# A retention kernel with a bilinear feed-forward: the first load of q and of k as two DMAs each

## The chip, the cores and the metric

The kernel runs on 1 core of one Trainium2 chip. The metric is the device time of one execution in microseconds. Before the change it is 325.2 us, the median of 3 runs (325.12 to 325.22).

## The reference

```
q, k, v: [8 batches, 8 heads, 576 positions, 64]
scores = (1 / 8) * q @ k.T                             # per batch and head
gamma[h] = 1 - 2 ** (-5 - h)
D[h, i, j] = gamma[h] ** (i - j) where i >= j, else 0
attn = (scores * D[h]) @ v
x = attn with the heads side by side                   # [4608 tokens, 512]
out = ((x @ w_a) * (x @ w_b)) @ w_out                  # w_a, w_b: 512 x 1536, w_out: 1536 x 512
```

There is no softmax, so the decay factors can be pulled apart into one factor per query and one per key, and the keys of earlier positions can be folded into a state (k.T @ v).

## The kernel before

The whole of the work runs on one core in an order that is written out by hand. The feed-forward part goes over the tokens in blocks (512, 256, 256, then 512 each). For a block it makes `pa = x @ w_a` (line 794), which ACT copies to `ha` (line 802), and `pb = x @ w_b` (line 809), which DVE multiplies with `ha` to `hT` (line 814), and then `po = hT @ w_out` (line 828). Retention work for later tokens is put between the matmuls of these blocks through a list of due times.

Before the first block there is an opening. It handles the first 256 positions of batches 0 and 1 in four steps, each of one batch and four heads: `STEPS` (line 165) makes step 0 the heads 0 to 3 of batch 0, step 1 the heads 0 to 3 of batch 1, step 2 the heads 4 to 7 of batch 0, and step 3 the heads 4 to 7 of batch 1. For a step, `load_step` (line 154) brings q, k and v in float32 into `qf`, `kf` and `vf`: 128 partitions, two neighbouring positions and four heads in each, 256 KB. `cast_step` (line 311) makes them bfloat16 (`qkb`) on the engine named in the call, one instruction over all four heads; `values_step` (lines 319 and 321) multiplies v by a factor per key; `transpose_step` (line 329, copies in line 333) turns q and k; `score_step` (line 347, masked in line 355) makes the scores; `state_step` (line 374, copies in lines 386 to 391) makes the states; the output steps (lines 421, 437, 448) make `xT`, the input of the feed-forward part. `make_qs` (line 223) makes tables of factors on ACT. `warm` (line 855) issues matmuls on a tile of ones whose result nobody reads. POOL issues the weight loads (lines 264, 266, 269) between its casts. The first feed-forward matmuls on half a block are in `ffn_begin` and `begin_with` (line 771).

The loads of the four steps are the first instructions of the program. They are issued in this order, all from SP except the first k, which ACT issues:

```python
    for i, which in ((0, Q), (0, K), (0, V), (2, Q), (2, K), (1, K),
                     (1, Q), (2, V), (3, K), (3, Q), (1, V), (3, V)):
        load_step(*STEPS[i], which,
                  nc.scalar if (i, which) == (0, K) else nc.sync)
```

Behind its load of k, ACT makes the factors of the keys (line 213) and two of the tables; the four steps then run as lines 860 to 920 list them, in the order 0, 2, 1, 3. DVE casts q and k of step 0, POOL casts those of step 2 and the k of steps 1 and 3, ACT casts the q of steps 1 and 3. Every DMA has a completion semaphore; the program uses eight for the DMAs of SP and ACT, in turn, and a DMA that takes one for the second time waits for the one that had it before.

Of the kernel before, what the change touches and what calls it, by code (L numbers as in the profile page):

```python
# [18 lines left out]
def kernel(  # L19
# [10 lines left out]
    nc = tc.nc  # L30

    B, H, S, D = q.shape
    DM = H * D
# [104 lines left out]
    paired = {}  # L138
# [12 lines left out]
                    src[b, :, s0:s0 + m, :].rearrange("h s d -> s h d"))  # L151
            paired[n][i] = t

    def load_step(n, hh, which, on=nc.sync):

        if n not in paired:
            paired[n] = [stage.tile([128, 2 * DM], FP32, tag=name, name=name)
                         for name in ("qf", "kf", "vf")]
        on.dma_start(  # L159
            paired[n][which][:, hh * DM:(hh + 1) * DM]  # L160
            .rearrange("p (h e) -> p h e", h=4),
            (q, k, v)[which][n, 4 * hh:4 * hh + 4, 0:256, :]
            .rearrange("h (p two) d -> p h (two d)", two=2))

    STEPS = [(0, 0), (1, 0), (0, 1), (1, 1), (2, 0), (2, 1)]
    Q, K, V = 0, 1, 2
    for i, which in ((0, Q), (0, K), (0, V), (2, Q), (2, K), (1, K),
                     (1, Q), (2, V), (3, K), (3, Q), (1, V), (3, V)):
        load_step(*STEPS[i], which,
                  nc.scalar if (i, which) == (0, K) else nc.sync)  # L170

# [757 lines left out]
    for i, which in ((4, Q), (4, K), (4, V), (5, Q), (5, K), (5, V)):  # L931
        load_step(*STEPS[i], which)
# [135 lines left out]
```

## Time and profile before

| | |
|---|---|
| time, median of 3 runs | 325.2 us |
| the profiled execution: its own time | 325.43 us |
| its span | 323.7 us |
| PE busy | 314.0 us (97%) |
| DVE, ACT, POOL busy | 165.4, 131.5, 118.8 us |
| moved by DMA | 50.90 MB, mean 157 GB/s |
| DMAs of `qf` from SP, 256 KB each | 32, median 4.7 us from issue to landing |
| granted TensorE clock | 1.00 |

The span is counted from the first to the last instruction of the core; 1.73 us of the profiled execution's own time lie around it. PE, DVE, ACT and POOL are the tensor, vector, scalar and GpSimd engines, PEld the weight loads of PE, SP the engine that only issues and waits. SPq and ACTq are the issuing of DMAs on SP and ACT, which is not counted as busy time. L12 is line 12 of the kernel before. In a timeline a row gives the start in us, the duration, the engine, the line, what is written and read, the shapes, and in brackets how long the engine was idle just before and what ended that. In a table of stretches each row has the stretch, its length, the busy time of PE, PEld, DVE, ACT and POOL (with the number of instructions), the granted clock, the mean busy share of the 16 DMA engines (it can pass 1 where packets overlap) and GB/s. A busy PE is not a PE at its peak.

### The profile page before, as it was taken

The page shows a single profiled execution, that of the slowest core. Times are in us where ns is not written, and L with a number is a line of the kernel's source. Part 1 is how long each engine was busy: PE and PEld are TensorE (multiplying, and loading weights), DVE is VectorE, ACT ScalarE, POOL GpSimd, SP SyncE. Part 2 cuts the span into 40 slices and gives each one's busy share as a digit, 9 for nine tenths or more (in the row PEclk, how much of TensorE's full clock was granted, in tenths as well). Part 3 has the DMA queues.
Part 4 walks back from the last instruction along what each step waited for, and adds up shares of the span by engine and source line. Part 5 has one row for each costly group of instructions (what it writes and reads, how often), then busy time and mean ns, then how long its engine had stood idle before and what let it go on. Part 6 is the DMA issues. An engine that isn't in the chain of part 4 may idle for free.

```text
span 323.7 us, 8631 instructions
## 1 busy us (share of the span) xinstructions
PE 314.0 (97%) x3573; PEld 164.4 (51%) x3611; DVE 165.4 (51%) x294; ACT 131.5 (41%) x293; POOL 118.8 (37%) x158
## 2 busy tenths in 40 slices
PE   7899999999999999999999999999999999999996
PEld 3564457778444554444454545454445444444444
DVE  5744445665546754835374626562566256514321
ACT  7735753463435523533253324442433343313321
POOL 4990077574755274447165305450530000000000
PEclk9999999999999999999999999999999999999999
DMA  8999999999999999999999169935840520031013
GB/s 216 255 196 207 259 231 189 200 176 206 174 221 223 195 208 206 269 222 263 175 197 216 52 163 198 207 74 144 194 86 19 104 76 2 2 97 32 1 23 108
DMA packets 145431, 50.90 MB, mean 157 GB/s; under 512 B 126704, under 2 KB 140912, under 8 KB 145392
## 3 DMA queue, kind: packets, MB, share of 16 engines
q1 hardware_dynamic: 140112, 45.37, 68.4%
q0 software_dynamic: 4752, 4.72, 8.8%
q8 instruction: 28, 0.46, 0.6%
q10 hardware_dynamic: 528, 0.26, 0.3%
q14 instruction: 11, 0.09, 0.1%
HBM read 37.75 MB, written 9.44 MB: 146 GB/s over the span
## 4 chain that ended last, share of the span: by engine, by line
PE 92%; DMA 2%; SPq 2%; ACT 1%; issue 1%; DVE 1%; DVEq 0%
PE pb L809 29%; PE po L828 29%; PE pa L794 28%; DMA qf<-in_q_dram 2%; SPq L159 2%; PE sc L600 1%; PE o L628 1%; PE o L641 1%; PE kv L538 1%; PE pa L771 1%; ACT state_after L386 0%; ACT vb L319 0%; PE tp L329 0%; DVE hT L814 0%; ACT own L390 0%
## 5 line engine op out<-in xcount | busy, mean ns | idle before, releaser
L814 DVE TENSOR_TENSOR hT<-ha,pb 128x512 bf16<-128x512 bf16 (+1 forms) x120 | 75.9, 633 | 94.8 <-PE pb L809 86.6
L802 ACT CAST ha<-pa 128x512 bf16<-128x512 f32 (+1 forms) x120 | 64.8, 543 | 115.9 <-PE pa L794 109.9
L809 PE MATMUL pb<-xT,wb_sb 128*128 128x512 bf16 (+1 forms) x474 | 111.2, 357 | 0.5
L794 PE MATMUL pa<-xT,wa_sb 128*128 128x512 bf16 (+1 forms) x452 | 106.9, 356 | 1.2 <-issue 0.6
L828 PE MATMUL po<-wo_sb,hT 128*128 128x512 bf16 (+2 forms) x442 | 94.7, 367 | 1.7 <-issue 1.4
L809 PEld LDWEIGHTS <-wb_sb 128*128 128x128 bf16 x480 | 47.0, 98 | 46.6 <-issue 0.3
L794 PEld LDWEIGHTS <-wa_sb 128*128 128x128 bf16 x468 | 45.0, 98 | 44.4 <-issue 0.2
L828 PEld LDWEIGHTS <-hT 128*128 128x128 bf16 x456 | 42.7, 98 | 47.2
L484 POOL CAST qkb<-qf 64x1024 bf16<-64x1024 f32 x15 | 15.5, 1031 | 64.4 <-DMA qf<-in_q_dram 55.1
L495 POOL TENSOR_TENSOR vb<-vf,vs 128x1024 bf16<-128x1024 f32 (+1 forms) x17 | 28.9, 1700 | 13.3 <-DMA vf<-in_v_dram 6.1
L839 DVE COPY osb<-po 128x512 f32<-128x512 f32 (+2 forms) x17 | 11.1, 653 | 43.0 <-PE po L828 43.0
L837 ACT COPY osb<-po 128x512 f32<-128x512 f32 (+1 forms) x21 | 12.0, 573 | 43.4 <-PE po L828 40.5
L484 POOL CAST qkb<-kf 64x1024 bf16<-64x1024 f32 (+1 forms) x17 | 16.4, 966 | 16.7 <-DMA kf<-in_k_dram 16.5
L563 DVE TENSOR_TENSOR sums<-kv,sums 128x256 f32<-128x256 f32 x44 | 18.7, 424 | 2.8 <-PE kv L538 0.8
L609 DVE TENSOR_TENSOR sT<-sc,mask 128x512 bf16<-128x512 f32 x30 | 19.4, 681 | 0.0
L488 POOL CAST qkb<-kf 64x512 bf16<-64x512 f32 (+1 forms) x34 | 18.7, 579 | 1.0
L488 POOL CAST qkb<-qf 64x512 bf16<-64x512 f32 x30 | 17.6, 615 | 0.6
L567 ACT CAST states<-sums 64x512 bf16<-64x512 f32 x26 | 16.0, 617 | 0.3
L654 DVE TENSOR_TENSOR xT<-o,qs 128x512 bf16<-128x512 f32 x24 | 15.4, 682 | 1.5 <-PE o L641 1.5
L311 POOL CAST qkb<-kf 128x512 bf16<-128x512 f32 x5 | 3.1, 617 | 16.9 <-DMA kf<-in_k_dram 16.9
L355 DVE TENSOR_TENSOR sT<-sc,mask_s 128x1024 bf16<-128x1024 f32 x6 | 7.2, 1222 | 1.3 <-PE sc L347 1.2
L855 PE MATMUL w<-ones 128*128 128x512 bf16 x17 | 6.3, 482 | 1.5 <-DVE idxp_f L204 1.5
(88 smaller groups left out, 163.5 us busy)
## 6 DMA issues: line engine op xcount, KB each, us to landing
qf<-in_q_dram SPq DMA_DIRECT2D x32, 256.0 KB, 4.7
vf<-in_v_dram SPq DMA_DIRECT2D x32, 256.0 KB, 5.2
kf<-in_k_dram SPq DMA_DIRECT2D x31, 256.0 KB, 4.8
out_dram<-osb SPq DMA_DIRECT2D x25, 256.0 KB, 3.2
out_dram<-osb SPq DMA_DIRECT2D x21, 128.0 KB, 2.6
wo_sb<-in_moe_w_out_dram POOLq DMA_DIRECT2D x3, 512.0 KB, 16.7
qf<-in_q_dram SPq DMA_DIRECT2D x8, 128.0 KB, 3.2
kf<-in_k_dram SPq DMA_DIRECT2D x8, 128.0 KB, 3.5
```

The lines of the kernel that those rows point to most:

```text
L484: nc.gpsimd.tensor_copy(qkb[0:64, w, e], t[0:64, e])
L488: nc.gpsimd.tensor_copy(to[:, :, 1 - r], fro[:, :, r])
L495: nc.gpsimd.tensor_tensor(vb[:, e].rearrange("p (h d) -> p h d", d=D), t[:, e].rearrange("p (h d) -> p h d", d=D), decay[:, at], op=ALU.mult)
L563: nc.vector.tensor_tensor(sums[:, i], own, prev, op=ALU.add)
L567: nc.scalar.copy(to(half(1 - r)), fro(half(r)))
L609: nc.vector.tensor_tensor(sT[:, on].rearrange("p c k s -> p (c k) s"), sc[:, on].rearrange("p c k s -> p (c k) s"), mask3.unsqueeze(1).to_ ...
L654: nc.vector.tensor_tensor(x_of(t0, 128).rearrange("p c (a s) -> p c a s", a=2), o[:, :, :, kp].rearrange("p a c s -> p c a s"), qs[:, :, s ...
L794: nc.tensor.matmul(pa[:, 0:n], wa_sb[:, c, fs], xT[:, c], start=(c == 0), stop=(c == NC - 1))
L802: nc.scalar.copy(ha[:, 0:n], pa[:, 0:n])
L809: nc.tensor.matmul(pb[:, 0:n], wb_sb[:, c, fs], xT[:, c], start=(c == 0), stop=(c == NC - 1))
L814: nc.vector.tensor_tensor(hT[:, F, 0:n], has[F][:, 0:n], pb[:, 0:n], op=ALU.mult)
L828: nc.tensor.matmul(po[:, 0:width], hT[:, F, u * 128:(u + 1) * 128], wo_sb[:, F, cols], start=(F == 0), stop=(F == NF - 1))
```

## The change

`load_step` gets a number of parts, and issues one DMA for each: `parts=2` makes two DMAs of two heads (128 KB) each, to the two halves of the same tile. It is 2 for the q and the k of step 0, and 1 for every other load. Both DMAs of q are issued from SP and both of k from ACT, one behind the other, in the places where the whole loads stood. Nothing else of the program's order differs; the two casts that read these tiles wait for both DMAs, and since two more semaphores are taken at the start, the first load that has to wait for a semaphore used before is that of q for step 1 instead of that of k for step 3.

```diff
-    def load_step(n, hh, which, on=nc.sync):
+    def load_step(n, hh, which, on=nc.sync, parts=1):
...
-        on.dma_start(
-            paired[n][which][:, hh * DM:(hh + 1) * DM]
-            .rearrange("p (h e) -> p h e", h=4),
-            (q, k, v)[which][n, 4 * hh:4 * hh + 4, 0:256, :]
-            .rearrange("h (p two) d -> p h (two d)", two=2))
+        for h in range(0, 4, 4 // parts):
+            hs = slice(4 * hh + h, 4 * hh + h + 4 // parts)
+            on.dma_start(
+                paired[n][which][:, 128 * hs.start:128 * hs.stop]
+                .rearrange("p (h e) -> p h e", h=4 // parts),
+                (q, k, v)[which][n, hs, 0:256, :]
+                .rearrange("h (p two) d -> p h (two d)", two=2))
...
         load_step(*STEPS[i], which,
-                  nc.scalar if (i, which) == (0, K) else nc.sync)
+                  nc.scalar if (i, which) == (0, K) else nc.sync,
+                  2 if i == 0 and which in (Q, K) else 1)
```

## The prediction

> **What bounds the kernel now.** I read the page first, then the timeline of the first 20 us, the chain of waits inside that stretch, and the DMA traffic cut into short stretches. The page:
>
> ```profile
> span 323.7 us, 8631 instructions
> PE 314.0 (97%) x3573; PEld 164.4 (51%) x3611; DVE 165.4 (51%) x294; ACT 131.5 (41%) x293; POOL 118.8 (37%) x158
> ...
> PE 92%; DMA 2%; SPq 2%; ACT 1%; issue 1%; DVE 1%; DVEq 0%
> ```
>
> PE carries 92% of the chain that ended last. Only some 4% of it, about 14 us, is DMA and SP's queue, and the chain in order of time puts all of that at the start: SP's issues from 0.80 to 6.56 us, then one q load (5.51 us) up to 12.07. From 16.81 us on PE runs the feed-forward matmuls with hardly a gap, so whatever moves 16.81 moves the end by the same amount. The change touches only what lies ahead of it. The timeline of the opening, all engines:
>
> ```profile
> 0.80 0.48 ACTq L159 DMA_DIRECT2D kf<-in_k_dram  x1
> 0.80 0.45 SPq L159 DMA_DIRECT2D qf<-in_q_dram  x1
> 1.31 0.49 SPq L159 DMA_DIRECT2D vf<-in_v_dram  x1
> ...
> 3.50 1.26 SPq L159 DMA_DIRECT2D qf<-in_q_dram  x1
> ...
> 4.43 0.43 DVE L311 CAST qkb<-qf 128x512 bf16<-128x512 f32 x1 [1.14 <-DMA qf<-in_q_dram]
> 4.86 0.43 DVE L311 CAST qkb<-kf 128x512 bf16<-128x512 f32 x1
> ...
> 5.35 0.59 ACT L333 COPY qkT<-tp 128x512 bf16<-128x512 bf16 x1 [0.90 <-PE tp L329]
> ...
> 6.80 0.61 POOL L311 CAST qkb<-qf 128x512 bf16<-128x512 f32 x1 [3.73 <-DMA qf<-in_q_dram]
> ...
> 9.38 0.62 ACT L311 CAST qkb<-qf 128x512 bf16<-128x512 f32 x1 [1.11 <-DMA qf<-in_q_dram]
> ...
> 12.09 0.62 ACT L311 CAST qkb<-qf 128x512 bf16<-128x512 f32 x1 [0.22 <-DMA qf<-in_q_dram]
> ...
> 16.81 2.79 PE L771 MATMUL pa<-xT,wa_sb 128*128 128x256 bf16 x24
> ```
>
> Each stage starts when a load lands: the first q at 4.43, the q of step 2 at 6.80, of step 1 at 9.38, of step 3 at 12.09. SP stops issuing freely at its sixth load: 1.26 us for one issue where the earlier ones took 0.45 to 0.51. From there the DMA engines, not SP, set the pace. How fast they run (second number the length of the stretch, the last two DMA share and GB/s):
>
> ```profile
> 1.90:2.40 0.50, 0.50 (x3) 0.20 (x2) 0.36 (x6) 0.50 (x1) 0.43 (x2) 1.00 0.40 121
> 2.40:2.90 0.50, 0.50 (x3) 0.22 (x2) 0.45 (x2) 0.49 (x4) 0.45 (x2) 1.00 0.77 211
> 2.90:3.40 0.50, 0.50 (x3) 0.18 (x2) 0.39 (x1) 0.50 (x8) 0.17 (x1) 1.00 1.08 324
> 3.40:3.90 0.50, 0.50 (x3) 0.15 (x1) 0.00 (x0) 0.50 (x3) 0.00 (x0) 1.00 1.15 342
> 3.90:4.40 0.50, 0.50 (x2) 0.15 (x1) 0.00 (x0) 0.50 (x2) 0.00 (x0) 1.00 1.15 345
> 4.90:6.00 1.10, 1.05 (x10) 0.56 (x10) 0.61 (x2) 0.65 (x2) 0.00 (x0) 1.00 1.17 291
> ```
>
> Nothing moves before 1.9 us, the first microsecond runs at 121 and 211 GB/s, and then the engines are full. So the opening is a full pipe of DMA with a soft start, and only the soft start and the bytes can move it.
>
> **The change, part by part.** *What it does not do.* Both casts of step 0 remain one instruction over all four heads; in the changed program each waits for two semaphores instead of one (one more semaphore instruction on DVE each; SP's rows show 0.017 us for one). So no computation can begin on the first two heads: the earliest gain is an earlier landing of the second half.
>
> *Bytes and packets.* The same 512-byte pieces move. The two queues of the opening carried 5808 and 528 packets for eleven loads and one, so 528 each, 16 of them the small closing ones. Two more DMAs add 32 packets over 16 engines, two per engine. A busy engine takes about 0.9 us for the 33 packets of one load (256 KB at 290 GB/s), or 0.027 us per packet: +0.05 us.
>
> *SP's extra issue.* One more issue ahead of the first v load and everything behind it. A q load of 128 KB elsewhere was issued in 0.37 us at the fastest, the whole one here in 0.45: I take 0.40 with the 0.04 between issues, so v goes out at about 1.7 instead of 1.31, and each load to the fifth is 0.4 to 0.5 later. At the sixth SP used to stand 0.75 us (1.26 − 0.51) longer than its issue needs; the delay ends in that standing time. It is hidden as long as the engines have work: by 4.40 us they moved 0.5 × (121+211+324+342+345) = 672 KB, by 4.90 some 0.82 MB, while 1.54 MB were issued by 3.46. The cover is over 2 us of traffic. Without the cover it would cost its 0.4 to 0.5 us in full.
>
> *A new wait on SP.* The program takes eight completion semaphores in turn, so the load of q for step 1 and that of v for step 2 now wait until the first halves have landed, and all later loads stand behind them in SP's queue; ACT's cast at 9.38 and POOL's product at 10.43 need them. The whole k landed 4.0 us after its issue, at 4.8; its first half must be there before. At worst the issue starts at 4.8 and ends at 5.3 instead of 4.76, with 0.7 MB or 2.5 us of earlier loads still to move: nothing.
>
> *ACT's extra issue.* The second half of k holds ACT for 0.4 to 0.5 us ahead of its table load, the eight exponentials and two tables of factors. ACT then idles 0.90 us before 5.35, so its copy is not delayed. If that second issue had to stand in line for over 0.9 us, the copy, the scores and DVE's work at 6.80 would slip by the rest.
>
> *The soft start.* Against 1.15 later, the DMA share was 0.40 and 0.77: (0.75 + 0.38) × 0.5 = 0.57 us of traffic lost. ACT's k was issued at the same 0.80 as q, yet in the queue counts its packets begin some 0.5 us after q's first: none up to 2.3 us, 4 from 2.3 to 2.5. Smaller first DMAs may reach all engines, and the second queue, sooner. The gain lies between 0 and 0.57, the loss is the rival below. I take a quarter, −0.15: only the first of the two waves is halved, and the queues have the same descriptors to go through.
>
> *Sum.* +0.05 − 0.15 = −0.10 us on the landing of everything from v on, and on 16.81. The first gate there is ACT, busy from 12.09 to 16.81 without a break after only 0.22 us of idle time; its cast follows the landing. The second is the first weight load, issued by POOL at 9.07 right behind its cast of a k load; it took 7.7 us, so it lands at 16.8, and it shifts with that cast. Both follow the stream, so the shift survives. The profiled execution took 325.43 us, its span 323.7 and 1.73 around it; 325.43 − 0.10 = 325.33. The median is 0.23 lower, 325.2, so the forecast is 325.1.
>
> The Trainium skill speaks against the change: "DMA: Bandwidth & Descriptors", section "Rules for kernel authors", says that many small transfers are to be coalesced, and that two transfers to disjoint halves aren't worth it because they serialize on the same 16 engines. Its section on the anatomy of one DMA gives a fixed cost of about 2.0 us (for the GpSimd path), so that two more in a row would by the page put the time some 2 us up if nothing overlapped them. The row above disagrees with that as a price, since SP's first five issues followed each other at some 0.55 us while the engines were filling.
>
> **Rivals.** *Slower: a fixed time per DMA on the way to the engines.* The 0.5 us between q's and k's first packets may be the time that one DMA takes to be spread, whatever its size, with both queues in one line. Four halves then take 2.0 us where two wholes took 1.0, and v comes 1.0 us later. For it: equal issue at 0.80, the lag of 0.5, and issue times that hardly shrink with size (0.37 against 0.45). Against: the backlog. By 4.40 us 672 KB had moved, 160 KB more than the first q and k; losing those costs 160/290 = 0.55 us, and without any backlog it is 1.0. With the 0.05: 325.8 to 326.25. It decides once a half takes more than about 0.3 us to be spread; at 0.25 the four take what the two took. A late first q also eats the 0.22 us of slack on ACT, which lies within this price.
>
> *Faster: the whole soft start goes.* If the engines are full from the first packet, 0.57 us return, and with the first packet earlier by the shorter issue (0.08) it is 0.65: 324.55 to 324.7. For it: the engines are idle more than half of 1.9 to 2.4. Against: the bytes per issue are halved in just that stretch.
>
> *No effect.* The casts wait for both halves, the pipe is full either way: 325.2. It lies inside the forecast.
>
> **How the numbers follow.** A measurement of this kernel can tell about 0.2%, 0.65 us, from no change. The forecast, −0.10, with its bounds of −0.5 and +0.55 has 0.54 together with no effect. The slower rival gets 0.34; its lower end is still within 0.65 us, and downstream slips could carry it over, so I put 0.30 beyond. The faster one gets 0.12, and reordered waits downstream of it 0.04 more: 0.16 beyond. The likeliest case alone spans 324.7 to 325.75. The range takes in the faster rival's end and the slower one's full price: 324.4 to 326.4.
>
> **What would show it.** Right: SP's load of q for step 1 again ends its issue near 4.8 us, ACT's casts start within 0.2 us of 9.38 and 12.09, and PE's first feed-forward matmul within 0.3 of 16.81. The slower rival: DMA share below 1 past 3.4 us, and the casts of steps 1 to 3 later by one and the same 0.5 to 1.0. The faster one: over 250 GB/s by 2.4 us, and the casts all earlier. ACT's second issue over 0.9 us, or a copy at 5.35 that waits for ACT itself, would make the ACT step wrong. A shift of the end unlike that of 16.81 would make the reading of the rest wrong.

## The result and the profile after

The changed kernel took 326.43 us, the median of 6 runs (325.98 to 326.76), against 325.16 us for the kernel before on the same chip (6 runs, 324.99 to 325.25). The ratio is 1.0039, 95% interval 1.0026 to 1.0052: 0.39% slower, which is the side that the forecast did not favour, and 0.03 us above the range. The profiled execution of after took 326.76 us with a span of 325.0; that of before 325.43 with 323.7. So the profiled pair differs by 1.33 us, the medians by 1.27.

The page of after: span, engines, and the shares of the chain that ended last.

```profile
span 325.0 us, 8673 instructions
PE 318.1 (98%) x3611; PEld 164.7 (51%) x3611; DVE 165.5 (51%) x294; ACT 131.5 (40%) x293; POOL 118.5 (36%) x158
...
PE 91%; DMA 4%; SPq 2%; DVE 1%; issue 0%; POOL 0%; DVEq 0%
```

PE still carries the chain. DMA holds 4% of it where it held 2%: a load of `w_a` of 7.21 us has come into it (below). PE's count differs (3611 against 3573) although both programs have the same matmuls; some records are missing before. The opening of after, in the timeline (start, duration, engine, line, what; in brackets the idle time just before and what ended it; lines after the diff are three higher than before):

```profile
0.80 1.03 ACTq L161 DMA_DIRECT2D kf<-in_k_dram  x2
0.80 0.97 SPq L161 DMA_DIRECT2D qf<-in_q_dram  x2
1.81 0.47 SPq L161 DMA_DIRECT2D vf<-in_v_dram  x1
...
4.09 0.61 SPq L161 DMA_DIRECT2D qf<-in_q_dram  x1
...
4.39 0.43 DVE L314 CAST qkb<-qf 128x512 bf16<-128x512 f32 x1 [1.10 <-DMA qf<-in_q_dram]
4.73 0.42 DVE L314 CAST qkb<-kf 128x512 bf16<-128x512 f32 x1
5.31 0.59 ACT L336 COPY qkT<-tp 128x512 bf16<-128x512 bf16 x1 [0.31 <-PE tp L332]
...
7.60 0.61 POOL L314 CAST qkb<-qf 128x512 bf16<-128x512 f32 x1 [4.54 <-DMA qf<-in_q_dram]
...
10.20 0.62 ACT L314 CAST qkb<-qf 128x512 bf16<-128x512 f32 x1 [1.55 <-DMA qf<-in_q_dram]
...
12.90 0.62 ACT L314 CAST qkb<-qf 128x512 bf16<-128x512 f32 x1 [0.23 <-DMA qf<-in_q_dram]
...
17.61 2.78 PE L774 MATMUL pa<-xT,wa_sb 128*128 128x256 bf16 x24
```

The halved loads themselves land earlier: q's cast at 4.39 (4.43 before), k's at 4.73 (4.86). Everything behind them is late by one amount: the casts of steps 2, 1 and 3 by 0.80, 0.82 and 0.81 us. PE's first feed-forward matmul starts at 17.61 instead of 16.81, again +0.80. The DMA traffic in the same stretches as were shown of before (the last two numbers are the engines' busy share and GB/s):

```profile
1.90:2.40 0.50, 0.50 (x3) 0.20 (x2) 0.36 (x6) 0.50 (x1) 0.43 (x2) 1.00 0.59 170
2.40:2.90 0.50, 0.50 (x3) 0.22 (x2) 0.45 (x2) 0.50 (x1) 0.45 (x2) 1.00 1.01 290
2.90:3.40 0.50, 0.50 (x3) 0.18 (x2) 0.39 (x1) 0.49 (x4) 0.16 (x1) 1.00 1.09 325
3.40:3.90 0.50, 0.50 (x3) 0.15 (x1) 0.00 (x0) 0.50 (x7) 0.00 (x0) 1.00 1.12 304
3.90:4.40 0.50, 0.50 (x3) 0.15 (x1) 0.01 (x1) 0.50 (x3) 0.00 (x0) 1.00 0.86 211
4.40:4.90 0.50, 0.36 (x3) 0.03 (x2) 0.50 (x2) 0.50 (x2) 0.00 (x0) 1.00 0.70 174
4.90:6.00 1.10, 1.10 (x10) 0.53 (x10) 0.61 (x2) 0.69 (x2) 0.00 (x0) 1.00 0.94 274
```

One stretch of before, for comparison:

```profile
4.40:4.90 0.50, 0.46 (x2) 0.00 (x0) 0.46 (x2) 0.05 (x1) 0.00 (x0) 1.00 1.18 299
```

The soft start did get better (170 and 290 GB/s where it was 121 and 211). But the full pipe is gone: from 3.9 to 4.9 us the engines run at 211 and 174 GB/s, where they ran at 345 and 299. By 6.0 us after has moved 0.5 × (170+290+325+304+211+174) + 1.1 × 274 = 1038 KB against 1141 KB before: 103 KB, or 0.36 us at 290 GB/s. That is less than half of 0.80, and most of it is soon made up: from 6.0 to 8.0 us after moves 321 GB/s, before 290.

**How a load lands.** The completion semaphore of every load gets 16 increments, one from each DMA engine when it has done its share, and the trace has the time of each. A load has landed with the last. (The Trainium skill says so too: "DMA: Bandwidth & Descriptors", section "Why a DMA increments its semaphore by 16 and not by 1": the engines finish independently, and only the full 16 means that all data has landed. It gives no size for the spread.) First and last engine, and the mean of the 16, in us:

| load | before | after |
|---|---|---|
| first v | 5.23 to 5.76 | 4.81 to 6.14 |
| q, step 2 | 6.13 to 6.67 | 5.77 to 7.47 |
| k, step 2 | 7.06 to 7.57 | 6.58 to 8.37 |
| k, step 1 | 7.94 to 8.46, mean 8.15 | 7.42 to 9.30, mean 8.26 |
| last v | 13.36 to 13.93 | 12.81 to 15.21 |

Before, the 16 engines work through each of the twelve loads within 0.51 to 0.57 us of each other. After, they have come apart to 1.70 us by q of step 2, and stay 1.76 to 1.88 apart over the next seven loads. For k of step 1 the first engine is 0.52 us *earlier* than before, the mean 0.11 later, the last 0.84 later; its cast (8.51 to 9.35) moved with the last. So the bytes are hardly late; one part of each load is. Since each engine takes about 0.9 us for its share of a load and has the next load's share queued, one that is behind has no pause in which to catch up. (Loads over other queues can be wide without the change: the first `w_a` load, which POOL issues, lands over 1.75 us before and 1.70 after.) The count of small packets shows the same, since each engine closes each load with one packet under 512 bytes. Before, in the stretches 7.3 to 7.6, 7.6 to 7.9 and 7.9 to 8.2 us:

```profile
DMA packets 180, 0.09 MB, mean 287 GB/s; under 512 B 12, under 2 KB 180, under 8 KB 180
DMA packets 177, 0.09 MB, mean 295 GB/s; under 512 B 4, under 2 KB 177, under 8 KB 177
DMA packets 170, 0.09 MB, mean 290 GB/s; under 512 B 0, under 2 KB 170, under 8 KB 170
```

After, in the same three stretches:

```profile
DMA packets 209, 0.11 MB, mean 352 GB/s; under 512 B 3, under 2 KB 209, under 8 KB 209
DMA packets 201, 0.10 MB, mean 326 GB/s; under 512 B 10, under 2 KB 201, under 8 KB 201
DMA packets 181, 0.09 MB, mean 304 GB/s; under 512 B 3, under 2 KB 181, under 8 KB 181
```

Both close 16 in 0.9 us, one load. Before they come in a burst and then none; after, in every stretch. The rate of 352 and 326 GB/s is the lost traffic coming back.

**From the casts to `pa`.** The +0.80 at the casts and the +0.80 at `pa` are not one shift that passed through. Before, PE's weights at `pa` waited 0.17 us for the first load of `w_a`:

```profile
16.80 1.75 PEld L771 LDWEIGHTS <-wa_sb 128*128 128x128 bf16 x17 [0.17 <-DMA wa_sb<-in_moe_w_a_dram]
```

That load landed at 16.76 before. In after it was issued 0.84 us later (9.91 against 9.07) and yet landed at 16.81, so it gates nothing there. What took its place is the last v load, the one with the widest gap between its engines (2.40 us), for which ACT stands 0.33 us:

```profile
15.23 1.06 ACT L322 ACTIVATE vb<-vf,vs 128x64 bf16<-128x64 f32 x4 [0.33 <-DMA vf<-in_v_dram]
```

From ACT's cast of step 3 to `pa` it took 4.71 us (12.90 to 17.61). In q_only below, where nobody stands for that v, it took 4.26. From these rows I estimate that the late cast alone would have put `pa` at 12.90 + 4.26 = 17.16, 0.35 late, and that the last v added the other 0.45.

**From +0.80 to +1.3.** The chain of after in order of time (start, length, what) has a new piece. Its last lines up to 25.2 us:

```profile
9.26 5.95 DMA vf<-in_v_dram
15.21 0.07 issue
15.27 0.56 POOL vb L324
15.83 7.21 DMA wa_sb<-in_moe_w_a_dram
23.04 0.05 issue
23.09 2.12 PE pa L797 x9
```

It is the same last v load. POOL multiplies it, and only then issues the second load of `w_a`: at 15.83 instead of 14.78. PE reaches line 797 with that weight missing, and the matmul starts at 23.09 instead of 22.03: +1.06, of which 0.26 is this wait. The two rows of before:

```profile
14.78 0.81 POOL L264 DMA_DIRECT2D wa_sb<-in_moe_w_a_dram  x1
...
22.03 3.62 PE L794 MATMUL pa<-xT,wa_sb 128*128 128x512 bf16 x16
```

The first `po` matmuls start 1.07 later (38.64 against 37.57), and the second group of them still 1.07 (62.98 against 61.91). The last 0.25 or so arise behind that; they lie within what one profiled execution differs from another, since from the start of that second group to the end of the span the kernels below took 261.6 to 262.3 us (before 261.8, after 262.1).

### The profile page after: what moved, and what is told of

Its sections match the earlier page's. It is cut to its first block, busy times and chain, and to the rows that moved or that the text cites. A ratio compares the mean times of both kernels' runs of the same rounds, so it can differ in the third digit from the quotient of the medians.

```text
span 325.0 us, 8673 instructions
## 1 busy us (share of the span) xinstructions
PE 318.1 (98%) x3611; PEld 164.7 (51%) x3611; DVE 165.5 (51%) x294; ACT 131.5 (40%) x293; POOL 118.5 (36%) x158
## 3 DMA queue, kind: packets, MB, share of 16 engines
q0 software_dynamic: 4752, 4.72, 9.0%
## 4 chain that ended last, share of the span: by engine, by line
PE 91%; DMA 4%; SPq 2%; DVE 1%; issue 0%; POOL 0%; DVEq 0%
PE po L831 29%; PE pa L797 28%; PE pb L812 28%; SPq L161 2%; DMA wa_sb<-in_moe_w_a_dram 2%; DMA vf<-in_v_dram 2%; PE o L631 1%; PE sc L603 1%; PE o L644 1%; PE kv L541 1%; PE tp L332 0%; DVE hT L817 0%; PE os L631 0%; DVE sums L566 0%; PE sc L350 0%
## 5 line engine op out<-in xcount | busy, mean ns | idle before, releaser
L797 PE MATMUL pa<-xT,wa_sb 128*128 128x512 bf16 (+1 forms) x468 | 108.8, 357 | 0.1
L831 PE MATMUL po<-wo_sb,hT 128*128 128x512 bf16 (+2 forms) x456 | 97.0, 368 | 0.0
```

Of the source, the lines that this page charges most:

```text
L797: nc.tensor.matmul(pa[:, 0:n], wa_sb[:, c, fs], xT[:, c], start=(c == 0), stop=(c == NC - 1))
L831: nc.tensor.matmul(po[:, 0:width], hT[:, F, u * 128:(u + 1) * 128], wo_sb[:, F, cols], start=(F == 0), stop=(F == NF - 1))
```

## The experiments

Every kernel below is the changed one with the edit shown, and each profile is one execution. An expectation numbers its theories. Theory 1 is that SP's later issue of v delays everything. Theory 2 is that every DMA ahead of v takes its own time on the way to the engines, so that their number counts. Theory 3 is that a second issue on ACT is what costs. Theory 4 is that the DMA engines run dry between the halves and the loads behind them, restart out of step, and stay so. Theory 5 is that the halves themselves put them out of step, whatever is queued.

The marks of all runs. "cast 2" and "cast 1" are the casts of q for step 2 (POOL) and step 1 (ACT); "engines" is the first to the last engine of the load of k for step 1, with the mean; "pa" is the first feed-forward matmul, "po" the second group of `po` matmuls.

| kernel | ratio to before, 95% interval | cast 2 | cast 1 | engines (mean) | pa | po |
|---|---|---|---|---|---|---|
| before | | 6.80 | 9.38 | 7.94 to 8.46 (8.15) | 16.81 | 61.91 |
| after | 1.0039 [1.0026, 1.0052] | 7.60 | 10.20 | 7.42 to 9.30 (8.26) | 17.61 | 62.98 |
| q_only | 1.0014 [1.0001, 1.0027] | 7.24 | 9.82 | 7.62 to 8.89 (8.20) | 16.79 | 61.88 |
| k_only | 1.0036 [1.0018, 1.0054] | 7.12 | 10.09 | 7.73 to 8.80 (8.01) | 18.18 | 63.63 |
| late_v | 1.0015 [1.0005, 1.0026] | 6.71 | 9.30 | 7.85 to 8.38 (8.10) | 16.37 | 61.47 |
| small_extra | 1.0029 [1.0018, 1.0040] | 7.13 | 9.70 | 8.28 to 8.76 (8.44) | 16.80 | 61.91 |
| changed_again | 1.0015 [0.9998, 1.0031] | 7.52 | 10.14 | 7.41 to 9.20 (8.35) | | |
| four_parts | 1.0044 [1.0024, 1.0064] | 8.10 | 10.70 | 8.13 to 9.78 (8.85) | 17.68 | 62.77 |
| split_step2 | 1.0003 [0.9988, 1.0018] | 6.84 | 9.39 | 7.93 to 8.47 (8.11) | 16.93 | 62.04 |
| v_on_act | 1.0034 [1.0014, 1.0054] | 6.12 | 9.32 | 7.93 to 8.40 (8.16) | 17.21 | 63.33 |
| dry_whole | 1.0058 [1.0029, 1.0088] | 7.13 | 10.92 | 8.34 to 10.00 (9.00) | 17.91 | 63.16 |
| dry_halves | 1.0057 [1.0035, 1.0079] | 7.04 | 10.79 | 8.15 to 9.87 (8.62) | 17.77 | 63.03 |
| k_late_v | 1.0006 [0.9996, 1.0015] | 7.12 | 9.74 | 7.57 to 8.80 (8.02) | 16.70 | 61.79 |
| v_on_pool | 1.0036 [1.0019, 1.0054] | 7.96 | 10.40 | 7.39 to 9.49 (8.37) | 17.72 | 62.81 |

The runs of the kernel before beside them had medians of 325.3, 325.72, 325.14 and 325.48 us and spread by 0.9 us or more (324.96 to 328.08 at the widest), where they had agreed within 0.26 at first. The small ratios are therefore weak, and the marks of the opening carry most verdicts. late_v and small_extra show the limit: by their marks they should be 0.4 us faster and equal, by their ratios they are 0.15% and 0.29% slower. The profiled execution was the fastest of all runs in both cases (324.97 and 325.91), and what the other runs lose is not in any trace.

### Each half of the change alone

```diff
-                  2 if i == 0 and which in (Q, K) else 1)
+                  2 if (i, which) == (0, Q) else 1)     # q_only; k_only: (0, K)
```

> Only the first q goes as two DMAs; the first k stays whole on ACT. Theory 1 (late issue: the v load and all behind it on SP are issued some 0.5 us later, and that passes through to the landings): v issued at 1.8 us instead of 1.31, the casts of steps 2, 1 and 3 some 0.8 us later as in the changed kernel (7.60, 10.20, 12.90), time 326.2 to 326.5. Theory 2 (every DMA, of whatever size and on whichever of the two queues, takes its own time on the way to the engines, so their number ahead of v counts): about half of the change, casts 0.4 us later, time 325.6 to 325.9.

> Only the first k goes as two DMAs, on ACT; SP issues the whole q, then v at 1.31 us as before. Theory 1 (late issue on SP): no change, casts at 6.80, 9.38 and 12.09 within 0.1 us, time 325.0 to 325.3. Theory 2 (number of DMAs ahead of v, both queues in one line): half of the change, casts 0.4 us later, 325.6 to 325.9.

Measured: 325.57 us (11 runs) and 326.89 us (7 runs) against 325.3. Both part the engines, to 1.27 and 1.07 us, and the casts of step 2 are 0.44 and 0.32 late, which add to 0.76 of the 0.80. For q_only that costs nothing at `pa` (16.79): the way from ACT's cast of step 3 to `pa` took 4.72 us before and takes 4.26 here (12.53 to 16.79). The first weights, for which PE waited before, landed at 16.29 here instead of 16.76, so the shift of 0.4 disappears. In the whole change it does not, by the wait for the last v that was shown above. k_only is the surprise: it loses more at `pa` than the whole change. Its timeline:

```profile
0.80 1.07 ACTq L161 DMA_DIRECT2D kf<-in_k_dram  x2
...
1.31 0.49 SPq L161 DMA_DIRECT2D vf<-in_v_dram  x1
...
5.76 0.43 DVE L314 CAST qkb<-kf 128x512 bf16<-128x512 f32 x1 [0.81 <-DMA kf<-in_k_dram]
```

SP's v went out at 1.31, ACT's second half of k a little later, and the half had to share the engines with v: v landed from 4.69 to 5.68, the half from 5.04 to 5.66. Step 0 then starts 0.9 us late and pushes ACT's own work (its cast at 12.09 starts at 13.70 for want of ACT, not of data). In the whole change this does not happen, since v is issued behind both halves of q. The traffic of k_only in one stretch:

```profile
4.40:4.90 0.50, 0.50 (x2) 0.00 (x0) 0.38 (x1) 0.50 (x2) 0.00 (x0) 1.00 1.27 252
```

The rate is lower than before (252 against 299 GB/s), but the share is not: it is 1.05 or more in every stretch from 2.4 us on, and yet the engines part.

### The same issue times without the halves

```diff
+    load_step(*STEPS[0], Q)                 # whole, from SP
+    load_step(*STEPS[0], K, nc.scalar)      # whole, from ACT
...
+        if c == 0:                          # behind DVE's second memset of lgp
+            nc.vector.memset(paired[0][V][0:1, 0:1], 0.0)
+            for i, which in ((0, V), (2, Q), (2, K), (1, K), (1, Q), (2, V),
+                             (3, K), (3, Q), (1, V), (3, V)):
+                load_step(*STEPS[i], which)
```

> q and k whole as before; SP's third load, v, waits for a memset of one element of its tile on DVE, so that v and all loads behind it are issued at about 1.8 us instead of 1.31, with no DMA more. Theory 1 (late issue): the casts of steps 2, 1 and 3 come 0.5 to 0.8 us later, time 325.7 to 326.4. Theory 2 (number of DMAs): the backlog hides it, casts within 0.15 us of before, time 325.0 to 325.4.

Measured: 325.62 us (9 runs) against 325.3. Two lines of its timeline:

```profile
1.76 0.39 SPq L161 DMA_DIRECT2D vf<-in_v_dram  x1
...
6.71 0.61 POOL L313 CAST qkb<-qf 128x512 bf16<-128x512 f32 x1 [3.65 <-DMA qf<-in_q_dram]
```

v is issued at 1.76 (1.81 in the changed kernel), the engines stay full (346 and 289 GB/s from 3.9 to 4.9 us) and in step (0.53 us), and no cast is late. Theory 1 falls: the later issue alone costs nothing, as the prediction said. (`pa` is even earlier, 16.37: the first `w_a` load landed at 16.33 here.)

### More DMAs beside whole loads

```diff
+    for on, at, x in ((nc.sync, 0, q), (nc.scalar, 1, k)):   # behind the whole q and k
+        on.dma_start(extra[:, at], x[0, 0:2, 0:256:2, 0:8]
+                     .rearrange("h p d -> p h d"))
```

Two loads that nobody reads take the places of the second halves. By this edit each has 256 pieces of 32 bytes, 8 KB, which is twice what the expectation says.

> q and k whole as before, and behind each of them on its queue one more DMA of 128 pieces of 32 bytes (4 KB) whose result nobody reads: as many DMAs as in the changed kernel, in the same places, with none of the halving. Theory 1 (late issue): v issued at 1.7 us, casts 0.4 to 0.7 us later, 325.6 to 326.3. Theory 2 (number of DMAs): like the changed kernel, casts 0.8 us later, 326.0 to 326.6. If instead it is the halving itself (smaller DMAs at the start), no change beyond 0.2 us.

Measured: 326.06 us (6 runs) against 325.3. The number of DMAs is that of the changed kernel and v is issued at 1.85 (1.81 there), but the engines are never short (share 1.36 and 1.18 from 3.9 to 4.9 us) and stay in step (0.48). All casts are 0.3 us late, the mean as much as the last engine (8.44 against 8.15): that is work, 544 more packets, and it is gone by `pa`. Two more DMAs do not by themselves part the engines, and Theory 2 falls in the form in which small DMAs count like large ones.

### The change again, and four parts

```diff
-                  2 if i == 0 and which in (Q, K) else 1)
+                  4 if i == 0 and which in (Q, K) else 1)     # four_parts
```

> The changed kernel once more, on one chip with the three others of this group, to see whether its profile repeats: q cast at 4.4 us, the first v late (ACT's products at 6.2), the DMA share under 0.9 between 3.9 and 4.9 us, and PE's first feed-forward matmul 0.5 to 0.9 us later than before. All theories expect 326.0 to 326.8; if the thin stretch near 4.4 us is missing while the time is the same, the lateness of v is not the cause.

> The first q and the first k as four DMAs of one head each. Theory 2 (number of DMAs ahead of the first v: it reaches the engines after they have run dry): the thin stretch is longer, v and the casts of steps 2, 1, 3 another 0.5 to 1.0 us later than in the changed kernel (POOL's first cast at 8.1 to 8.6), 326.9 to 327.8. Theory 3 (the second issue on ACT and the late k or late ACT work are what costs, not the loads behind): POOL's first cast stays near 7.6, while ACT, now with four issues, is done with its tables at about 6.0 and its first copy comes 0.6 to 0.9 us late; 326.8 to 327.6.

Measured: 326.36 us (13 runs) and 326.83 us (12 runs) against 325.72. The repetition shows the same marks (7.52, 10.14, engines 1.79 apart); its profiled execution took 330.51 us, the longest of the 13, the last v was complete only at 16.71 and `pa` started at 19.61, so nothing later is read from it. Its ratio alone would not tell it from no change. Four parts run the engines dry earlier (199 GB/s from 2.9 to 3.4 us, 123 from 3.9 to 4.4) and the casts come 1.3 us late, but the engines are no further apart than with two (1.65). So the gap grows with the parts, the spread does not. POOL's cast at 8.10 is against Theory 3, which had it near 7.6. The first load behind the gap, v, still lands within 0.43 us; the next, q of step 2, is 1.74 wide.

### Halves where a backlog stands

```diff
-                  2 if i == 0 and which in (Q, K) else 1)
+                  2 if i == 2 and which in (Q, K) else 1)
```

> The first q, k and v whole as before, and the q and the k of step 2, the fourth and fifth loads, as two DMAs each from SP. Theory 2 (it is the start, with nothing queued behind, that makes a further DMA cost): with a backlog the two more DMAs are hidden, casts within 0.2 us of before, 325.1 to 325.5. If every DMA costs a fixed time wherever it stands, the casts of steps 1 and 3 come 0.5 to 1.0 us later and the time is 325.8 to 326.4.

Measured: 325.81 us (12 runs) against 325.72, 1.0003. The same two tiles' worth of halves, but behind three whole loads: the casts of steps 2 and 1 at 6.84 and 9.39 (6.80 and 9.38), engines 0.54 apart, and the same 345 and 294 GB/s. Halving costs nothing where the engines have other work.

### The first v from the other queue

```diff
-                  nc.scalar if (i, which) == (0, K) else nc.sync,
-                  2 if i == 0 and which in (Q, K) else 1)
+                  nc.scalar if i == 0 and which in (K, V) else nc.sync,
+                  1)
```

> All loads whole; the first v is issued from ACT behind k, SP goes on with the q of step 2. ACT's table load comes as late as in the changed kernel (1.9 us). Theory 2: two queues with whole loads on each feed the engines longer at the 340 GB/s that two queues showed against 290 for one, so the casts of steps 2, 1 and 3 come 0.2 to 0.4 us earlier than before; 324.8 to 325.2. Theory 3 (a second issue on ACT is the cost): ACT's work and with it step 0 come late, 325.8 to 326.6.

Measured: 326.99 us (12 runs) against 325.72. The engines stay in step (0.47) and q of step 2 comes 0.7 us early (6.12), but v comes behind it (6.59 instead of 5.76), and ACT and DVE wait for v. Order, not pace, is what this kernel loses. Neither expectation of the time came true.

### Running dry on purpose

```diff
     nc.vector.memset(state_after, 0.0)
+    nc.vector.memset(paired[0][V][0:1, 0:1], 0.0)    # the first v can't be issued before this
+    for i, which in ((0, V), (2, Q), (2, K), (1, K), (1, Q), (2, V),
+                     (3, K), (3, Q), (1, V), (3, V)):
+        load_step(*STEPS[i], which)                  # q and k of step 0: whole / halved
```

> q and k whole; the first v and all loads behind it wait for DVE's memsets and are issued from about 3.4 us on, so that all engines are done with q and k (before: first to last engine 4.32 to 4.84 for k) about when v reaches them. Theory 4 (running dry puts the engines out of step, and they stay so: each load lands with its last engine): the closing packets of one load spread over 1 us or more instead of 0.52, as in the changed kernel. Theory 5 (the halving, with two short loads on each of two queues, puts them out of step): the spread stays near 0.5 us and all loads behind shift alike by 0.5 to 0.8 us. Either way 325.8 to 326.6.

> q and k as two DMAs each, as in the changed kernel, and the first v and all behind it issued only from about 3.4 us on, when nothing is left of the halves. Theory 4 (running dry puts the engines out of step): spread of 1 to 1.9 us, loads later than in the whole version by about 0.5 us. Theory 5 (it is v's descriptors going out while the halves are still being worked off that leaves some engines behind): with the halves gone, v starts on all engines afresh, spread near 0.5 us, the same landings as with whole loads and the same delay. 326.0 to 327.0.

Measured: 327.12 us (9 runs) with whole loads, 326.86 us (7 runs) with halves, against 325.14. Here no load of dry_whole is split, and SP issues v at 3.32. The traffic of dry_whole from 3.4 to 4.9 us, and from 6.7 to 7.6:

```profile
3.40:3.90 0.50, 0.50 (x3) 0.15 (x1) 0.00 (x0) 0.50 (x3) 0.00 (x0) 1.00 1.03 305
3.90:4.40 0.50, 0.50 (x2) 0.15 (x1) 0.00 (x0) 0.50 (x2) 0.00 (x0) 1.00 0.21 60
4.40:4.90 0.50, 0.50 (x2) 0.00 (x0) 0.41 (x2) 0.05 (x1) 0.00 (x0) 1.00 0.72 186
...
6.70:7.00 0.30, 0.30 (x17) 0.21 (x16) 0.10 (x1) 0.30 (x3) 0.00 (x0) 1.00 0.64 191
7.00:7.30 0.30, 0.30 (x17) 0.14 (x5) 0.00 (x0) 0.30 (x3) 0.17 (x1) 1.00 0.64 161
7.30:7.60 0.30, 0.30 (x17) 0.15 (x16) 0.28 (x1) 0.30 (x1) 0.30 (x1) 1.00 0.80 227
```

The engines of dry_whole end 1.66 us apart, those of dry_halves 1.72. Whole loads do it as halves do, so Theory 5 falls: no halving is needed. Theory 4 stands in part. The engines part where they run short, but not by running dry and starting again: the first two loads behind the deepest gap (share 0.21) still land within 0.52 and 0.51 us. The third, which passes the second lull, is 1.55 wide, and the later ones are 1.52 to 1.76. In that lull the loads were there on paper. At 6.7 us SP had issued six since 3.32, of which two had landed or were about to (v at 6.08, q of step 2 at 7.00), and yet the share was 0.64, where it was 1.17 before. A load that is issued is not yet a load that the engines have.

The trace has the time of every packet, and it adds one thing. Between 3.5 and 8 us the median packet of 512 bytes takes 0.027 to 0.033 us, but the kernels whose engines part have one to six packets that take 0.3 to 0.9 us (in k_only two, of 0.87 and 0.85, and they count in its share); before, late_v, small_extra and split_step2 have none. In dry_halves one of 0.91 starts at 7.06, during the load of k for step 2: 14 engines are through with that load by 7.74, the last at 8.97. Yet v_on_act has two, of 0.60 and 0.53, and stays in step. So held packets go with the parting, and whether they are its cause is not shown.

### Halving k alone, with v behind it

```diff
     load_step(*STEPS[0], Q)
-    load_step(*STEPS[0], K, nc.scalar)               # of late_v
+    load_step(*STEPS[0], K, nc.scalar, 2)            # the rest as in late_v
```

> q whole, k as two DMAs on ACT, and v issued at about 1.76 us instead of 1.31, so that k's second half (issued at 1.35) goes ahead of it. With k split alone its second half landed at 5.66 us, behind v. If the order of issue over both queues sets the order of service: k's second half lands near 4.5 and DVE's second cast is back at about 4.9 us, and v at 5.7 or later. The spread between the engines, 1.07 us with k split alone, stays over 0.8 if splitting at the start is what spreads them; time 325.5 to 326.3.

Measured: 325.25 us (10 runs) against 325.14, 1.0006. With v at 1.76, behind the second half of k, that half lands at 4.65 and its cast starts on time:

```profile
4.76 0.42 DVE L313 CAST qkb<-kf 128x512 bf16<-128x512 f32 x1
```

So k_only's large loss came from v's issue at the same time as the half's. What is left is the halving: mean landing 8.02 (0.13 earlier than before: the better soft start), last engine 8.80 (0.34 later), and the later casts vanish in front of `pa` (16.70). The engines end 1.23 us apart, as was expected if a split at the start spreads them; since they also ran at a share of 0.88 from 4.4 to 4.9 us, this run alone does not tell Theory 5 from Theory 4. It is no faster than the kernel before.

### The first v from POOL

```diff
-    for i, which in ((0, Q), (0, K), (0, V), (2, Q), (2, K), (1, K),
+    for i, which in ((0, Q), (0, K), (2, Q), (2, K), (1, K),
...
+    load_step(*STEPS[0], V, nc.gpsimd)               # behind POOL's second table of indices
```

> The changed kernel, with the first load of v issued by POOL (behind its second table of indices) instead of by SP, so that SP's next load, q of step 2, goes out where v did (about 1.8 us) and v goes out about 1.35 us on a queue of its own. Both first loads stay halved. Theory 4 (the engines run dry between the halves and the fifth load, come out of step there and stay so): v fills the gap; DMA share at 3.9 to 4.9 us at or above 1, first to last engine of the load of k of step 1 near 0.55 us, POOL's cast of step 2 (q) at 6.5 to 6.9, ACT's casts at 9.2 to 9.5 and 11.9 to 12.2, first feed-forward matmul at 16.4 to 16.9, time within 0.5 us of the kernel before. Theory 5 (halves themselves put the engines out of step, whatever is queued behind them): first to last engine over 1.2 us again, casts at 7.2 or later and 9.8 or later. If v's packets from POOL also come only at 4.6 us or later, the gap stays, and the run says nothing between the two.

Measured: 326.19 us (12 runs) against 325.48. POOL issued v from 1.46 to 2.38, and the gap stayed: 200 and 194 GB/s from 3.9 to 4.9 us. Neither v nor the q of step 2, which now had v's place on SP, filled it, and the engines came 2.10 us apart. By its own terms the run says nothing between the two theories. It does show that a third queue is no cure.

No version was faster than the kernel before.

## Why the prediction was wrong

**The step that failed** is "SP's extra issue": the delay "is hidden as long as the engines have work", and "The cover is over 2 us of traffic". The term was put at nothing, and the last engine of the loads behind came 0.8 us late. The cover was counted in bytes that SP had issued. At 4.09 us SP and ACT of the changed kernel had issued six loads, 1.57 MB; by 4.40 the engines had moved 650 KB of it, and with 0.9 MB outstanding on paper they ran at a share of 0.86 and then 0.70. The halves were done by 4.50, sooner than the wholes (4.84), and v, issued at 1.81, was not at work on all engines by then: the first was through with it at 4.81, the last at 6.14. dry_whole shows the same fault of reckoning without any split.

**What the sum had no term for** is the engines' step. It treated the 16 as one pipe, in which lost traffic returns. In that picture the forecast was not far off: the mean landing of k for step 1 moved by +0.11 us where the sum said −0.10, and a gain by the soft start shows where k alone is halved (the mean is 0.13 to 0.14 earlier in k_only and k_late_v, where −0.15 was put), though not where q alone is (0.05 later in q_only). But a load is used when its last engine is through, and that moved by +0.84.

**Point by point.** *Packets*, +0.05: within what the runs can tell; small_extra, with 544 more instead of 32, lost 0.3. *The new wait on SP*, nothing: right, q of step 1 ended its issue at 4.70. *ACT's extra issue*, hidden: right, the copy starts at 5.31 with 0.31 us of idle time left of 0.90. *The size of an issue*: a half took 0.45 to 0.52 us to issue, as much as a whole, not 0.40; and the load at 95.1 us that was issued in 0.37 us moved 256 KB, not 128. *Both gates of 16.81 follow the stream*: wrong. The cast did, but the first `w_a` load, issued 0.84 later, landed only 0.05 later. A shift of up to 0.4 us vanished (q_only, k_late_v), and that +0.80 at the casts met +0.80 at `pa` is a coincidence, since part of the latter came from the last v. *What moves 16.81 moves the end alike*: wrong; another 0.26 came from the second load of `w_a`, which POOL issues behind the last v.

**The slower rival** gave the marks that came true: share below 1 past 3.4 us, the casts of steps 1 to 3 later by one amount between 0.5 and 1.0, and 325.8 to 326.25 us, a little under the 326.43 measured. That was luck in part: its mechanism, a fixed time to spread each DMA in one line over both queues, is not confirmed. The same number of DMAs in small_extra starved nobody, and in after the first half of k landed 0.23 us behind that of q. That v arrives late behind four short DMAs is common to both; the price came from the engines' step, which the rival did not have either.

**The rules of the Trainium skill** that were weighed ("DMA: Bandwidth & Descriptors", "Rules for kernel authors": coalesce; two transfers to disjoint partition halves aren't worth it) had the right sign for these loads, which are halved by heads and not by partitions. The estimate of some 2 us from that page's fixed cost did not come true, with +0.80 at the casts; where a backlog stood, halving neither cost nor gained anything (split_step2, 1.0003).

**What stays open.** Why the load of v that SP issued at 1.81 us was not at work on all engines when the halves ended, why a lull leaves some engines more than a microsecond behind (the trace does not name the engines) and why k_only parts them without its share falling below 1, and the few tenths behind the second group of `po`. An attempt to fill the gap from a third queue failed, so it was not shown in the changed kernel itself that the spread goes when the gap is filled; that is inferred from late_v, split_step2 and dry_whole.

## What to carry to other kernels

Count a DMA backlog in what the engines have, by the share and GB/s of short stretches, and not in what has been issued: here a share below 1 with loads outstanding went with engines out of step, and once, in k_only, a fall of the rate alone did. At the start of a program keep the first transfers long enough that the next ones have arrived before they end; a split that is free in mid-stream can starve the engines there. And read the landing of a load by its last engine, since a short lull can cost every later load more than the lull itself.

## What the hardware showed that was not expected

- The 16 DMA engines can come out of step and stay so as long as their queues are full: 0.5 us apart before, 1.76 to 1.88 after over seven loads in a row.
- They do so after a lull with whole loads too (1.66 us), and not at once: two loads passed in step (0.52, 0.51) before the third was 1.55 wide.
- Two loads issued at the same time from two queues shared the engines: k's second half (ACT, 1.32) landed at 5.66 beside v (SP, 1.31) at 5.68. With v issued at 1.76 the half landed at 4.65 and v at 6.10.
- Single packets of 512 bytes took 0.3 to 0.9 us, where the median is 0.027 to 0.033, in every kernel whose engines came out of step; in one kernel two of them did no harm.
- Issuing 128 KB took as long as 256 KB: 0.45 to 0.52 us against 0.45 to 0.51. In four_parts 64 KB took 0.39 to 0.46.
